# Linear attention with two branches on one core: query units of both branches in pairs of PSUM banks, single chunks of one weight load, and the last heads of both branches side by side

## The chip, the cores and the metric

The kernel runs on one core of a Trainium2 chip. The metric is the device time of one execution in microseconds (us); lower is better. All runs were fast, with a granted TensorE clock of 1.0. Within one call the kernels run on the same chip and share the runs of the kernel before. Each kernel was profiled in one of its executions; where profiles are compared below, it is one execution against one. A ratio is the mean time of a kernel's fast runs over the mean of the fast runs of the kernel before in the same rounds, with a 95% interval; it is therefore not quite the ratio of the medians that stand beside it. The span of a profile is about 1.3 us shorter than the time of the same run.

## The reference, cut to what matters

```python
# x: [1, 2048, 640] bf16; two branches A and B with their own wqkv [640, 1920] and wo [640, 640]; 32 heads of 20
g = sigmoid((x * gate_w).sum(-1, keepdims=True))
def branch(x, wqkv, wo):
    q, k, v = ...                                  # [1, 32, 2048, 20] each
    phi = lambda t: where(t > 0, t + 1, exp(t)) + 1e-6
    pq, pk = phi(q), phi(k)
    kv = einsum("bhsd,bhse->bhde", pk, v);  z = einsum("bhsd->bhd", pk)
    num = einsum("bhqd,bhde->bhqe", pq, kv)
    den = einsum("bhqd,bhd->bhq", pq, z)[..., None] + 1e-6
    return (num / den) merged over heads @ wo
return g * branch(A) + (1 - g) * branch(B)
```

## The kernel before

The work on TensorE goes in this order: keys of both branches (k), the products of phi(k) with x (g), the small products with the values (m), their products with wo (wp), then the queries in four blocks of 512 positions (q), the denominators (den), and the output matmuls (final). The wp rows go through DRAM to change their layout: WS is stored to the DRAM tensor wrows and loaded back as WPA or WPB. The reciprocal of the denominators takes the same road: RC is written to the DRAM tensor factor and read back as RX, spread over the heads. VectorE then multiplies phi(q) by RX.

The instructions are not written in the order in which an engine runs them. The kernel has its own list scheduler. At build time it gives each operation a duration from a small model, gives each engine a fixed order, and reserves PSUM banks. On the chip every engine runs its fixed order, and waits where a semaphore is late.

```python
WPLAG = 2

# loading of B's key weights: three transfers of 1, 2 and 2 chunks
for c0, c1 in ((0, 1), (1, 3), (3, 5)):
    dma("SP", "wkB%d" % c0, WK["B"][:, c0:c1, :], weights("B", D, c0, c1), writes=[...], us=0.55 * (c1 - c0))

def q_unit(X, b, k):                       # one branch, one PSUM bank, 512 columns
    tile = _Tile(1)
    ...
    mms("q%s%d%d" % (X, b, k), steps, [...], [(tile,)], NC * 518, after=gone[X])
    sch.op("ACT", ... e.activation(ek(), PS[:, tile.banks[0], :], ACT.Exp) ...)
    sch.op("DVE", ... e.tensor_scalar(ek(), ek(), 1.0, EPS, op0=ALU.min, op1=ALU.add) ...)
    sch.op("DVE", ... e.scalar_tensor_tensor(out=dst, in0=PS[...], scalar=0.0, in1=ek(), op0=ALU.max, op1=ALU.add) ...)

def wp_rows(X):                            # wsX, stored earlier by wp_store, holds the other rows
    dma("SP", "ws5" + X, ...)
    dma("SP", "wp" + X, WP[X][:, :, :], ..., reads=[("WD", X, 0), ("WD", X, 5)], writes=[("WP", X, k) for k in range(NC)], us=2.2)

def scale_q(b, dtile, pieces):
    sch.op("ACT", ... DN ...)              # copy the denominators out of PSUM
    sch.op("DVE", rec, 1740, ...)          # RC = 1 / DN
    dma("SP", "fw%d" % b, ...)             # factor <- RC
    dma("SP", "fr%d" % b, ..., reads=[("FD", b)], writes=[(xs,)], us=0.6)      # RX <- factor
    for j in range(pieces):
        for X in XS:
            sch.op("DVE", ... PQ[X] *= RX ...)

def queries(b):
    for X in XS:
        for k in range(NC):
            q_unit(X, b, k)
            q = 5 * (X == "B") + k - WPLAG
            if b == 1 and 0 <= q < 6:
                wp_unit("B", (q - 1) % 6)
                if q == 0: wp_rows("A")

queries(0); m_unit("B"); queries(1)
wp_store("B"); wp_rows("B")
d01 = dens(0); scale_q(0, d01, 2)
queries(2); queries(3)
...
```

## Time and profile before

| | |
|---|---|
| time, median | 190.74 us (190.50 to 191.07, 6 runs) |
| span of the profiled run | 189.7 us |
| TensorE / VectorE / ScalarE busy | 186.3 / 130.1 / 76.4 us |
| TensorE without a gap | 9.39 to 187.26 us |

The page of the kernel before, busy times and the chain that ended last:

```profile
PE 186.3 (98%) x1289; PEld 124.0 (65%) x1289; DVE 130.1 (69%) x275; ACT 76.4 (40%) x129; POOL 8.2 (4%) x14
PE 94%; DMA 3%; SPq 1%; DVE 0%; issue 0%; DVEq 0%
```

The chain in order of time (start, duration, what):

```profile
3.55 5.80 DMA WK<-in_B_wqkv_dram
...
9.39 177.87 PE ps L383 x1241
```

The busy share proves little by itself, because matmuls overlap and their ends are modelled. The starts do better. The timeline of TensorE in the queries (start, duration, engine, line, operation, operands, count):

```profile
95.31 5.56 PE L383 MATMUL ps<-XT,WQA 128*128 128x512 bf16 x25
100.71 5.56 PE L383 MATMUL ps<-XT,WQB 128*128 128x512 bf16 x25
```

25 matmuls of 512 columns start within 100.71 - 95.31 = 5.40 us, 216 ns each. The Trainium skill, "TensorE: Matmul & The Clock Gate", section "Wait — 56ns, not 53.3ns?", puts a warm matmul at its columns over 2.4 GHz plus about 2.5 ns, 215.8 ns here; the trace agrees. So TensorE is at this floor in the queries, and the chain shows no gap of it from 9.39 to 187.26 us.

SyncE issues the transfers of this stage, in a fixed order (start and duration of the issue, not of the transfer):

```profile
118.72 0.34 SPq L372 DMA_DIRECT2D wrowsB<-WS  x1
123.72 0.35 SPq L372 DMA_DIRECT2D WPB<-wrowsB  x1
125.59 2.31 SPq L372 DMA_DIRECT2D factor<-RC  x2
128.70 1.70 SPq L372 DMA_DIRECT2D RX<-factor  x2
```

And VectorE, where the multiplies of block 0 stand between the sums of the query units:

```profile
129.82 1.28 DVE L752 SCALAR_TENSOR_TENSOR FE<-ps,EK 128x512 bf16<-128x512 f32 x2
131.47 3.03 DVE L811 TENSOR_TENSOR FE<-FE,RX 128x1280 bf16<-128x1280 bf16 x4 [0.37 <-DMA RX<-factor]
134.42 0.49 DVE L747 TENSOR_SCALAR EK<-EK 128x512 bf16<-128x512 bf16 x2
```

The bracket says that VectorE stood idle for 0.37 us before the multiplies, until RX had landed. TensorE felt nothing of it: its matmuls show no late start there.

### The profile page before, as it was taken

The numbers are of one execution on the slowest core, as the hardware profiler recorded it, in microseconds if no ns is written. First come the engines' busy times: TensorE is split into PE (matmuls) and PEld (weight loads), VectorE is DVE, ScalarE is ACT, GpSimd is POOL, SyncE is SP. The second block draws the span as 40 slices with busy tenths as digits, with TensorE's granted clock in tenths as the row PEclk, the third lists the DMA queues.
The fourth block names the chain that finished last, engine by engine and source line by source line (L and its number), as shares of the span: only waits on it lengthen the run. The fifth ranks groups of instructions, "written<-read, shape, count | busy, mean of one in ns | idle before, by whom it ended". The sixth has DMA issues, their size and how long they took to land.

```text
span 189.7 us, 3209 instructions
## 1 busy us (share of the span) xinstructions
PE 186.3 (98%) x1289; PEld 124.0 (65%) x1289; DVE 130.1 (69%) x275; ACT 76.4 (40%) x129; POOL 8.2 (4%) x14
## 2 busy tenths in 40 slices
PE   8999999999999999999999999999999999999995
PEld 3565555555788888888855666455556677777774
DVE  1398989898600009996179997899999959833324
ACT  2255555555311112203255478565553522331332
POOL 8900000000000000000000000000000000000000
DMA  6999699991011111112144004665000173211212
GB/s 184 282 229 202 183 381 371 352 241 43 0 35 38 35 35 38 35 35 38 35 86 111 5 22 173 165 223 171 0 0 3 43 228 92 97 66 46 73 69 69
DMA packets 31936, 21.49 MB, mean 113 GB/s; under 512 B 16818, under 2 KB 31666, under 8 KB 31922
## 3 DMA queue, kind: packets, MB, share of 16 engines
q1 hardware_dynamic: 31490, 20.80, 39.4%
q10 hardware_dynamic: 432, 0.49, 0.8%
q8 instruction: 10, 0.16, 0.4%
q14 instruction: 4, 0.03, 0.1%
HBM read 12.05 MB, written 5.31 MB: 91 GB/s over the span
## 4 chain that ended last, share of the span: by engine, by line
PE 94%; DMA 3%; SPq 1%; DVE 0%; issue 0%; DVEq 0%
PE ps L383 94%; DMA WK<-in_B_wqkv_dram 3%; SPq L372 1%; DVE OL L862 0%; DVEq L276 0%
## 5 line engine op out<-in xcount | busy, mean ns | idle before, releaser
L383 PE MATMUL ps<-WK,XT 128*128 128x512 bf16 (+2 forms) x250 | 44.1, 337 | 0.4 <-DMA WK<-in_B_wqkv_dram 0.2
L383 PE MATMUL ps<-XN,FE 128*128 128x320 bf16 x320 | 44.3, 300 | 0.0
L383 PEld LDWEIGHTS ps<-XN,FE 128*128 128x128 bf16 x320 | 37.5, 117 | 6.0
L383 PEld LDWEIGHTS ps<-WK,XT 128*128 128x128 bf16 x250 | 24.0, 98 | 20.2 <-DMA WK<-in_B_wqkv_dram 1.1
L743 ACT ACTIVATE EK<-ps 128x512 bf16<-128x512 f32 x40 | 23.9, 597 | 18.4 <-PE ps L383 17.4
L563 ACT ACTIVATE EK<-ps 128x512 bf16<-128x512 f32 (+1 forms) x42 | 21.4, 526 | 16.2 <-PE ps L383 16.2
L752 DVE SCALAR_TENSOR_TENSOR FE<-ps,EK 128x512 bf16<-128x512 f32 x40 | 26.8, 688 | 0.7
L856 ACT ACTIVATE TS<-ps,GA 128x640 f32<-128x640 f32 (+2 forms) x18 | 13.1, 735 | 29.3 <-PE ps L383 29.3
L383 PE MATMUL ps<-WPB,FE 128*128 128x320 bf16 (+1 forms) x165 | 24.5, 295 | 0.0
L383 PE MATMUL ps<-WPA,FE 128*128 128x320 bf16 (+1 forms) x165 | 24.5, 295 | 0.0
L573 DVE SCALAR_TENSOR_TENSOR FE<-ps,EK 128x512 bf16<-128x512 f32 (+1 forms) x42 | 23.9, 597 | 0.5
L862 DVE SCALAR_TENSOR_TENSOR OS<-ps,GA,TS 128x640 bf16<-128x640 f32 x15 | 13.0, 870 | 15.2 <-PE ps L383 15.2
L383 PE MATMUL ps<-XT,WQA 128*128 128x512 bf16 x100 | 22.8, 380 | 0.0
L383 PE MATMUL ps<-XT,WQB 128*128 128x512 bf16 x100 | 22.7, 379 | 0.0
L600 ACT ACTIVATE GS<-ps 128x640 bf16<-128x640 f32 x10 | 7.0, 704 | 37.0 <-PE ps L383 37.0
L383 PEld LDWEIGHTS ps<-WPA,FE 128*128 128x128 bf16 x165 | 16.0, 98 | 6.2
L383 PEld LDWEIGHTS ps<-WPB,FE 128*128 128x128 bf16 x165 | 15.8, 98 | 6.2 <-ACT TS L856 0.4
L383 PEld LDWEIGHTS ps<-XT,WQB 128*128 128x128 bf16 x100 | 11.7, 117 | 9.2
L383 PEld LDWEIGHTS ps<-XT,WQA 128*128 128x128 bf16 x100 | 11.6, 118 | 9.4 <-issue 0.4
L705 DVE SCALAR_TENSOR_TENSOR GP<-XN,GWB 128x640 bf16<-128x640 bf16 x16 | 13.3, 828 | 4.1 <-PE ps L383 3.6
L567 DVE TENSOR_SCALAR EK<-EK 128x512 bf16<-128x512 bf16 (+1 forms) x42 | 11.4, 272 | 3.1
L811 DVE TENSOR_TENSOR FE<-FE,RX 128x1280 bf16<-128x1280 bf16 (+1 forms) x20 | 12.6, 686 | 0.9 <-DMA RX<-factor 0.9
(52 smaller groups left out, 80.8 us busy)
## 6 DMA issues: line engine op xcount, KB each, us to landing
out_dram<-OS SPq DMA_DIRECT2D x15, 160.0 KB, 1.8
XN<-in_A_x_dram SPq DMA_DIRECT2D x3, 640.0 KB, 8.4
factor<-RC SPq DMA_DIRECT2D x4, 256.0 KB, 2.6
RX<-factor SPq DMA_DIRECT2D x4, 256.0 KB, 3.0
WVA<-in_A_wqkv_dram SPq DMA_DIRECT2D x1, 800.0 KB, 10.8
WQA<-in_A_wqkv_dram SPq DMA_DIRECT2D x1, 800.0 KB, 12.2
WVB<-in_B_wqkv_dram SPq DMA_DIRECT2D x1, 800.0 KB, 11.2
WQB<-in_B_wqkv_dram SPq DMA_DIRECT2D x1, 800.0 KB, 12.2
```

The costliest lines, as they stand in the source:

```text
L372: ins = e.dma_start(dst() if callable(dst) else dst, src() if callable(src) else src, transpose=transpose)
L383: ins = pe.matmul(o, l, r, start=a, stop=z, tile_position=tp, skip_group_check=True)
L563: "ACT", lambda e, ps=ps, ek=ek: e.activation(ek(), ps(), ACT.Exp), _act_ns(n), reads=[(tile,)], writes=[(es,)],
L567: "DVE", lambda e, ek=ek: e.tensor_scalar(ek(), ek(), 1.0, EPS, op0=ALU.min, op1=ALU.add), _dve_ns(n, 4),
L573: return e.scalar_tensor_tensor(out=out, in0=two(ps()), scalar=0.0, in1=two(ek()), op0=ALU.max, op1=ALU.add)
L600: "ACT", lambda e: e.activation(GS[:, k, :].rearrange("p (h f) -> p h f", f=HALF), pair(tile, HALF), ACT.Copy),
L705: lambda e, t=t: e.scalar_tensor_tensor(out=GP[:, :], in0=XN[:, t, 0:D], scalar=1.0, in1=GWB[:, :], op0=ALU.mult, op1=ALU.mult, accum_out= ...
L743: "ACT", lambda e: e.activation(ek(), PS[:, tile.banks[0], :], ACT.Exp), _act_ns(512), reads=[(tile,)],
L752: lambda e: e.scalar_tensor_tensor(out=dst, in0=PS[:, tile.banks[0], :], scalar=0.0, in1=ek(), op0=ALU.max, op1=ALU.add),
L811: return e.tensor_tensor(out=v, in0=v, in1=RX[:, xs.slot, 512 * x + w * j : 512 * x + w * j + w].unsqueeze(1).to_broadcast([128, NC, w]), ...
L856: "ACT", lambda e: e.activation(t_ap(), acc(), ACT.Copy, scale=GA[:, 0, t : t + 1]), _act_ns(hi - lo),
L862: lambda e: e.scalar_tensor_tensor(out=o_ap(), in0=acc(), scalar=GA[:, 1, t : t + 1], in1=t_ap(), op0=ALU.mult, op1=ALU.add),
```

## The change

Its intent is to save work on VectorE and ScalarE with fewer, larger instructions, to let TensorE start on the first chunks of B's key weights sooner, and to run ten small matmuls in pairs. The diff has five parts, cut to their core:

```diff
-WPLAG = 2
+WPAT = ((1, 0), (1, 1), (1, 2), (1, 3), (1, 4), (2, 0))
 # 1. single chunks of B's WK, on two issuing engines
-        for c0, c1 in ((0, 1), (1, 3), (3, 5)):
-            dma("SP", "wkB%d" % c0, ...)
+        for c in range(NC):
+            load_wk(("SP", "ACT")[c % 2], "B", c)
 # 2. query units of A and B together: two banks, one Exp, one clamp, one sum
-        def q_unit(X, b, k):
-            tile = _Tile(1)
+        def q_pair(b, k):
+            tile = _Tile(2)
+            ... 10 matmuls, 5 for each branch, then Exp, clamp and sum of 1024 columns
 # 3. the last heads (40 columns) of A are computed with B's, side by side on two halves of the array
-                        for g in (0, 1) if q < 5 else (last,):
+                r = [step(X, tiles[0], q, g, j) for q in range(5) for j in range(NC) for g in (0, 1)]
+                if X == "B":
+                    r += [step(Y, tiles[1 - g], 5, g, j) for j in range(NC) for g, Y in enumerate(XS)]
 # 4. the wp units of B: one behind each of six pairs, in place of one behind each of six single units
-                    q = 5 * (X == "B") + k - WPLAG
-                    if b == 1 and 0 <= q < 6:
-                        wp_unit("B", (q - 1) % 6)
+                q_pair(b, k)
+                for i, p in enumerate(WPAT):
+                    if p == (b, k):
+                        wp_unit("B", (i - 1) % 6)
+                        if i == 5:
+                            wp_store("B")
+                            wp_rows("B")
 # 5. denominators copied out at once; the scaling of block 0 listed behind the queries of block 2
-        d01 = dens(0)
-        scale_q(0, d01, 2)
+        d0, d1 = dens(0)
         queries(2)
+        scale_q(0, d0, 2)
```

More of the change, by code (lines that the diff above doesn't have):

```diff
@@ L409, in load_x, with load_wk @@
             dma(eng, "xn%d" % t, XN[:, t, 0:D], xin[128 * t : 128 * t + 128, :], writes=[("XN", t)], us=0.25)
-        def load_wk(eng, c):
-            dma(eng, "wkA%d" % c, WK["A"][:, c, :], weights("A", D, c, c + 1)[:, 0, :], writes=[("WK", "A", c)], us=0.25)
+        def load_wk(eng, X, c):
+            dma(eng, "wk%s%d" % (X, c), WK[X][:, c, :], weights(X, D, c, c + 1)[:, 0, :], writes=[("WK", X, c)], us=0.25)
         load_x("SP", 0)
-        load_wk("ACT", 0)
+        load_wk("ACT", "A", 0)
         load_x("SP", 1)
-        load_wk("ACT", 1)
-        load_wk("SP", 2)
-        load_wk("ACT", 3)
-        load_wk("SP", 4)
-        for c0, c1 in ((0, 1), (1, 3), (3, 5)):
-            dma(
-                "SP", "wkB%d" % c0, WK["B"][:, c0:c1, :], weights("B", D, c0, c1), writes=[("WK", "B", c) for c in range(c0, c1)],
-                us=0.55 * (c1 - c0),
-            )
+        load_wk("ACT", "A", 1)
+        load_wk("SP", "A", 2)
+        load_wk("ACT", "A", 3)
+        load_wk("SP", "A", 4)
+        for c in range(NC):
+            load_wk(("SP", "ACT")[c % 2], "B", c)
         for t0, t1 in ((2, 4), (4, 8), (8, 12), (12, 16)):
@@ L484, in transpose_x @@
                 )
-        ring = {"ek": _Ring(NEK), "dn": _Ring(2), "rx": _Ring(2), "os": _Ring(NOS), "ts": _Ring(NTS)}
+        ring = {"ek": _Ring(NEK), "eq": _Ring(NEK // 2), "dn": _Ring(2), "rx": _Ring(2), "os": _Ring(NOS), "ts": _Ring(NTS)}
         def phi_k(X, t, tile):
@@ L622, in m_unit, with step, mask @@
         def m_unit(X):
-            tile = _Tile(1)
-            last = XS.index(X)
-            def steps():
-                r = []
-                for q in range(6):
-                    w = 12 if q < 5 else 8
-                    for j in range(NC):
-                        for g in (0, 1) if q < 5 else (last,):
-                            at = D * j + 120 * q + 60 * g * (q < 5)
-                            r.append((
-                                PS[64 * g : 64 * g + 64, tile.banks[0], 60 * q : 60 * q + NC * w], WV[X][:, at : at + 64],
-                                GT[X][:, j, :, 24 * q + 12 * g * (q < 5) : 24 * q + 12 * g * (q < 5) + w], j == 0, j == NC - 1, (0, 64 * g),
-                            ))
-                return r
-            mms("m%s" % X, steps, [("GT", X, k) for k in range(NC)] + [("WV", X), ("WVP", X)], [(tile,)], 25 * 75 + 400)
-            for q0, q1, g, w in ((0, 5, 0, 12), (0, 5, 1, 12), (5, 6, last, 8)):
+            tiles = [_Tile(1)] + [_Tile(1)] * (X == "B")
+            def step(Y, tile, q, g, j):
+                w, lo = (12, 12 * g) if q < 5 else (8, 0)
+                at = D * j + 120 * q + DH * lo // 4
+                return (
+                    PS[64 * g : 64 * g + 64, tile.banks[0], 60 * q : 60 * q + NC * w], WV[Y][:, at : at + 64],
+                    GT[Y][:, j, :, 24 * q + lo : 24 * q + lo + w], j == 0, j == NC - 1, (0, 64 * g),
+                )
+            def steps():
+                r = [step(X, tiles[0], q, g, j) for q in range(5) for j in range(NC) for g in (0, 1)]
+                if X == "B":
+                    r += [step(Y, tiles[1 - g], 5, g, j) for j in range(NC) for g, Y in enumerate(XS)]
+                return r
+            ys = XS if X == "B" else ("A",)
+            mms(
+                "m%s" % X, steps, [("GT", Y, k) for Y in ys for k in range(NC)] + [("WV", Y) for Y in ys] + [("WVP", Y) for Y in ys],
+                [(t,) for t in tiles], (len(tiles) + 9) * 190 + 240,
+            )
+            parts = [(0, 0, 5, 0, 12), (0, 0, 5, 1, 12)]
+            if X == "B":
+                parts = [(1, 5, 6, 0, 8), (0, 5, 6, 1, 8)] + parts
+            for i, q0, q1, g, w in parts:
                 n = DH * (w // 4)
-                def mask(e, q0=q0, q1=q1, g=g, w=w, n=n):
+                def mask(e, i=i, q0=q0, q1=q1, g=g, w=w, n=n):
                     p0 = 64 * g
@@ L648, in mask @@
                         out=MB[p0 : p0 + n, q0:q1, 60 * g : 60 * g + n].rearrange("p q (i k) -> p q k i", k=NC),
-                        in0=PS[p0 : p0 + n, tile.banks[0], 60 * q0 : 60 * q0 + n * (q1 - q0)].rearrange("p (q k i) -> p q k i", k=NC, i=w),
+                        in0=PS[p0 : p0 + n, tiles[i].banks[0], 60 * q0 : 60 * q0 + n * (q1 - q0)].rearrange(
+                            "p (q k i) -> p q k i", k=NC, i=w
+                        ),
                         in1=m.unsqueeze(1).to_broadcast([n, q1 - q0, NC, w]), op=ALU.mult,
@@ L653, in m_unit @@
                 sch.op(
-                    "DVE", mask, _dve_ns(n * (q1 - q0)), reads=[(tile,), ("CB",)], writes=[("M", q) for q in range(q0, q1)],
+                    "DVE", mask, _dve_ns(n * (q1 - q0)), reads=[(tiles[i],), ("CB",)], writes=[("M", q) for q in range(q0, q1)],
                     name="mm%s" % X,
@@ L722, in gates, with eq, eq2 @@
             )
-        def q_unit(X, b, k):
-            tile = _Tile(1)
-            es = _Tile(1, ring["ek"])
-            def ek():
-                return EK[:, es.slot, 0:512]
-            dst = PQ[X][:, k, 512 * b : 512 * b + 512]
+        def q_pair(b, k):
+            tile = _Tile(2)
+            es = _Tile(1, ring["eq"])
+            def eq():
+                return EK[:, :, :].rearrange("p n f -> p (n f)")[:, 1280 * es.slot : 1280 * es.slot + 1024]
+            def eq2():
+                return eq().rearrange("p (x s) -> p x s", x=2)
+            dst = FE[:, :, S * k + 512 * b : S * k + 512 * b + 512]
@@ L732, in q_unit @@
             span = range(S * k + 512 * b, S * k + 512 * b + 512)
-            over = [("F", X, w, t) for w in ("k", "k5") for t in range(span[0] // D, span[-1] // D + 1)]
+            over = [("F", X, w, t) for X in XS for w in ("k", "k5") for t in range(span[0] // D, span[-1] // D + 1)]
             def steps():
                 return [
-                    (PS[:, tile.banks[0], :], WQ[X][:, c, k : D : NC], XT[:, c, 512 * b : 512 * b + 512], c == 0, c == NC - 1, None)
-                    for c in range(NC)
-                ]
@@ L741, in q_unit @@
-            mms("q%s%d%d" % (X, b, k), steps, [("XTC", t, c) for t in range(4 * b, 2) for c in range(NC)] + [("XT", t) for t in range(max(2, 4 * b), 4 * b + 4)] + [("WQ", X)], [(tile,)], NC * 518, after=gone[X])
+                    (PS[:, tile.banks[x], :], WQ[X][:, c, k : D : NC], XT[:, c, 512 * b : 512 * b + 512], c == 0, c == NC - 1, None)
+                    for x, X in enumerate(XS) for c in range(NC)
+                ]
+            xt = [("XTC", t, c) for t in range(4 * b, 2) for c in range(NC)] + [("XT", t) for t in range(max(2, 4 * b), 4 * b + 4)]
@@ L742, in q_unit @@
+            o = mms("q%d%d" % (b, k), steps, xt + [("WQ", X) for X in XS], [(tile,)], 2 * NC * 518, after=gone["B"])
+            sch.op("ACT", lambda e: e.activation(eq2(), pair(tile, 512), ACT.Exp), _act_ns(1024), reads=[(tile,)], writes=[(es,)], name="eq%d%d" % (b, k))
             sch.op(
-                "ACT", lambda e: e.activation(ek(), PS[:, tile.banks[0], :], ACT.Exp), _act_ns(512), reads=[(tile,)],
-                writes=[(es,)], name="eq%s%d%d" % (X, b, k),
+                "DVE", lambda e: e.tensor_scalar(eq(), eq(), 1.0, EPS, op0=ALU.min, op1=ALU.add), _dve_ns(1024, 4),
+                reads=[(es,)], writes=[(es,)], name="tq%d%d" % (b, k),
@@ L745, in q_unit @@
             )
             sch.op(
-                "DVE", lambda e: e.tensor_scalar(ek(), ek(), 1.0, EPS, op0=ALU.min, op1=ALU.add), _dve_ns(512, 4),
-                reads=[(es,)], writes=[(es,)], name="tq%s%d%d" % (X, b, k),
-            )
-            sch.op(
-                "DVE",
-                lambda e: e.scalar_tensor_tensor(
-                    out=dst, in0=PS[:, tile.banks[0], :], scalar=0.0, in1=ek(), op0=ALU.max, op1=ALU.add
-                ),
-                _dve_ns(512), reads=[(tile,), (es,)], writes=[("PQ", X, k, b)] + over, name="sq%s%d%d" % (X, b, k),
-            )
+                "DVE", lambda e: e.scalar_tensor_tensor(out=dst, in0=pair(tile, 512), scalar=0.0, in1=eq2(), op0=ALU.max, op1=ALU.add),
@@ L758, in dens @@
+                _dve_ns(1024), reads=[(tile,), (es,)], writes=[("PQ", X, k, b) for X in XS] + over, name="sq%d%d" % (b, k),
+            )
+            return o
         def dens(b0):
@@ L778, in dens, with scale_q @@
             )
-            return dtile
-        def scale_q(b, dtile, pieces):
-            ds = _Tile(1, ring["dn"])
-            lo = 256 * (b % 2)
-            sch.op(
-                "ACT",
-                lambda e: e.activation(DN[:, ds.slot, :], PS[:, dtile.banks[0], lo : lo + 256], ACT.Identity, bias=EP[:, 0:1]), _act_ns(256),
-                reads=[(dtile,), ("EP",)], writes=[(ds,)], name="dn%d" % b,
-            )
+            ds = []
+            for b in (b0, b0 + 1):
+                d = _Tile(1, ring["dn"])
+                ds.append(d)
+                sch.op(
+                    "ACT",
+                    lambda e, d=d, lo=256 * (b - b0): e.activation(
+                        DN[:, d.slot, :], PS[:, dtile.banks[0], lo : lo + 256], ACT.Identity, bias=EP[:, 0:1]
+                    ),
+                    _act_ns(256), reads=[(dtile,), ("EP",)], writes=[(d,)], name="dn%d" % b,
+                )
+            return ds
+        def scale_q(b, ds, pieces):
             def rec(e):
@@ L919, in queries @@
         def queries(b):
-            for X in XS:
-                for k in range(NC):
-                    q_unit(X, b, k)
-                    q = 5 * (X == "B") + k - WPLAG
-                    if b == 1 and 0 <= q < 6:
-                        wp_unit("B", (q - 1) % 6)
-                        if q == 0:
+            for k in range(NC):
+                q_pair(b, k)
+                for i, p in enumerate(WPAT):
+                    if p == (b, k):
+                        wp_unit("B", (i - 1) % 6)
+                        if i == 0:
                             wp_rows("A")
+                        if i == 5:
+                            wp_store("B")
+                            wp_rows("B")
         def finals(b):
@@ L938, in bass_gated_mix__linear_attn_block__linear_attn_block__prompt_kernel @@
         queries(1)
-        wp_store("B")
-        wp_rows("B")
-        d01 = dens(0)
-        scale_q(0, d01, 2)
+        d0, d1 = dens(0)
         queries(2)
+        scale_q(0, d0, 2)
         queries(3)
-        scale_q(1, d01, 2)
-        d23 = dens(2)
+        scale_q(1, d1, 2)
+        d2, d3 = dens(2)
         finals(0)
-        scale_q(2, d23, 2)
+        scale_q(2, d2, 2)
         finals(1)
-        scale_q(3, d23, 4)
+        scale_q(3, d3, 4)
         finals(2)
```

## The prediction

> **What bounds the kernel.** TensorE. The chain of waits has one unbroken piece of TensorE work, 177.87 of 189.7 us, from 9.39 to 187.26; before it 5.8 us of WK-of-B DMA, after it about 2.4 us of output. The page's busy share (98%) proves little, since matmul ends are modelled, so I used start-to-start times in the timeline: 25 query matmuls of 512 columns take 5.40 us (216 ns each), ten output matmuls of 320 columns 1.358 us (136 ns). The Trainium skill, "TensorE: Matmul & The Clock Gate", section "Wait — 56ns, not 53.3ns?", gives N/2.4 GHz plus about 2.5 ns for a warm matmul: 215.8 and 135.8 ns; the trace agrees. So after 9.39 us TensorE runs at its own rate; only fewer matmuls or a shorter start save time.
>
> **The change, costed.**
> 1. Query pairs. Still 200 matmuls of 512 columns, 43.2 us. From the groups, Exp takes 384/597/702 ns at 256/512/640 columns, the sum 415/688/825, the clamp 227/288/336. Estimates at 1024: Exp 1.02 us, clamp 0.42, sum 1.23. ScalarE saves 20 x 0.17 = 3.4 us, VectorE 20 x 0.30 = 6 us, both off the chain: VectorE is 96-99% busy at 120-150 us, yet TensorE does not wait there. Worth 0.
> 2. Cost of pairs: a pair is held for 2.16 us of matmuls plus about 3 us of Exp, clamp, sum and handover: 5.2 us against 2.16 us between pairs, so 2.4 of 4 pairs in use. With the m tiles, a wp tile or a den bank one pair less is left, when masks (1.03 us each) or reciprocals (1.75) come between. I allow 0 to 1 us of new TensorE stalls near 106-110, 120-123 and 142-148 us; expected 0.2.
> 3. Single WK chunks. TensorE loses 0.21, 0.31 and 0.41 us (late starts at 6.75, 8.43, 9.39) to WK. Chunks of 160 KB land about 0.45 us apart, so bytes, not issue, set the pace; two issuing engines share the same 16 DMA engines (the skill, "DMA: Bandwidth & Descriptors", section "Issuing engines are not separate DMA queues"). B's last byte stays near 9.3 us. But today chunks 3 and 4 land together at 9.345 and 14 matmuls follow; with single chunks 12 follow: 2 x 136 ns = 0.27 us saved, on the chain.
> 4. Last heads side by side. Five single 40-column matmuls start 32 ns apart in each branch; side by side two take those 32 ns. 5 x 32 = 0.16 us saved, on the chain.
> 5. wp of B ends later (near 121 us); WPB's way through DRAM (about 5 + 4 us) still ends before its use near 144 us.
>
> Sum: -0.27 - 0.16 + 0.2 = about -0.25; I say 190.4 us, 8 in 10 between 189.7 and 191.3. Faster by over 2%: 0.01; within 2%: 0.97; slower: 0.02.
>
> **Signs.** Right: query pairs 2.16 us apart; Exp near 1.02, sum near 1.23 us; VectorE busy near 124 us, ScalarE near 73; last B chunk landing at 9.0 to 9.6 us, then twelve 320-column matmuls. Wrong: TensorE waiting on VectorE or ScalarE inside 95-150 us for over 0.5 us in all (step 2), B's last chunk landing before 8.9 or after 9.8 us (step 3), a wait on WPB before the final matmuls (step 5).
>
> **What would upset it.** The kernel's list scheduler orders work by its own cost model; a badly placed mask or reciprocal could stall several pairs.

## The result, and the profile after

The kernel after takes 192.88 us in the median (191.86 to 193.56, 6 runs), the kernel before 190.74 us. The ratio is 1.0105 (1.0074 to 1.0137). So it is slower by about 1%, less than 2%, but outside the range of the prediction (189.7 to 191.3). Its runs also scatter three times as widely: 1.7 us against 0.6. The profiled run was the fastest of the six, with a span of 190.5 us.

The page of the kernel after:

```profile
PE 185.6 (97%) x1280; PEld 124.2 (65%) x1289; DVE 125.7 (66%) x235; ACT 73.0 (38%) x109; POOL 8.2 (4%) x14
PE 88%; DMA 6%; DVE 4%; issue 1%; ACT 0%; DVEq 0%
```

ScalarE saves what was forecast (3.4 us) and VectorE 4.4 us of the 6 forecast, and the chain now leaves TensorE. In order of time:

```profile
125.40 1.75 DVE RC L802
127.15 1.08 DVE FE L759
128.23 0.05 DVE EK L755
128.28 5.13 DMA factor<-RC
133.40 0.02 issue
133.42 2.78 DMA RX<-factor
136.20 0.02 issue
136.22 3.04 DVE FE L820 x4
139.26 0.67 DVE EK L755 x2
139.93 1.14 DVE FE L759
141.07 0.05 issue
141.12 7.79 PE ps L383 x50
```

Read it from the bottom. At 141.12 TensorE starts a query pair that waited for two free banks. They came free with the sum of an earlier pair (L759, ending at 141.07), that sum stood behind the four multiplies of block 0 (L820), and these waited for RX. RX waited for the write of the factor, which took 5.13 us. (The chain names VectorE, L759 and L755, for the 1.13 us before that write. The write needs neither: what ended at 128.23 was also SyncE's issue before it, as the SyncE view below shows.) The timeline of TensorE shows what it cost:

```profile
137.75 1.24 PE L383 MATMUL ps<-XT,WQA 128*128 128x512 bf16 x5
138.83 1.24 PE L383 MATMUL ps<-XT,WQB 128*128 128x512 bf16 x5
141.12 1.27 PE L383 MATMUL ps<-XT,WQA 128*128 128x512 bf16 x5 [1.05 <-DVE FE L759]
```

Five matmuls from 138.83 on take 5 x 216 ns, so the next could have started at 139.91. It starts 1.21 us later. (A group that shows x4, followed by a start 216 ns late, is a missing record and no gap; I don't count those.) VectorE and SyncE of the kernel after, in the same stage:

```profile
133.34 1.23 DVE L759 SCALAR_TENSOR_TENSOR FE<-ps,EK 128x1024 bf16<-128x1024 f32 x1
136.22 3.04 DVE L820 TENSOR_TENSOR FE<-FE,RX 128x1280 bf16<-128x1280 bf16 x4 [1.66 <-DMA RX<-factor]
139.17 0.76 DVE L755 TENSOR_SCALAR EK<-EK 128x1024 bf16<-128x1024 bf16 x2
```

```profile
122.89 0.34 SPq L372 DMA_DIRECT2D wrowsB<-WS  x1
127.88 0.35 SPq L372 DMA_DIRECT2D WPB<-wrowsB  x1
128.28 2.57 SPq L372 DMA_DIRECT2D factor<-RC  x2
133.42 1.12 SPq L372 DMA_DIRECT2D RX<-factor  x2
```

The store of B's rows is issued at 122.89 instead of 118.72, since its last wp unit now comes behind the first pair of block 2. SyncE can issue the load of WPB only when those rows have landed, at 127.88. The write of the factor is next in SyncE's order: RC was ready at 127.15 (end of L802 in the chain), but the write is issued at 128.28. Then the write and the load of WPB are under way together. The packets of the trace say how: from 128.3 to 131.6 the DMA engines moved packets of the load alone (109, none under 2 KB), and the write's 512-byte packets began at 131.64. So the write stood behind the load's data in SyncE's DMA queue, more than it moved beside it.

Counted from the first den matmul, RX of block 0 lands after 131.45 - 121.99 = 9.46 us in the kernel before, and after 136.20 - 123.58 = 12.62 us in the kernel after. The difference of 3.16 us has three parts: the write is issued 1.10 us later on this scale (4.70 against 3.60), it takes 2.04 us more (5.13 against 3.09), and the read is nearly the same (2.78 against 2.75).

### The profile page after: what moved, and what is told of

It is laid out like the page before. It is cut to its first block, busy times and chain, and to the rows that moved or that the text cites. A ratio compares the mean times of both kernels' runs of the same rounds, so it can differ in the third digit from the quotient of the medians.

```text
span 190.5 us, 3131 instructions
## 1 busy us (share of the span) xinstructions
PE 185.6 (97%) x1280; PEld 124.2 (65%) x1289; DVE 125.7 (66%) x235; ACT 73.0 (38%) x109; POOL 8.2 (4%) x14
## 4 chain that ended last, share of the span: by engine, by line
PE 88%; DMA 6%; DVE 4%; issue 1%; ACT 0%; DVEq 0%
PE ps L383 87%; DMA factor<-RC 3%; DMA XN<-in_A_x_dram 2%; DVE FE L820 2%; DMA RX<-factor 1%; DVE FE L759 1%; DVE RC L802 1%; PE ps L468 1%; DVE EK L755 0%; DVE OL L871 0%; ACT DN L791 0%; DVEq L276 0%
## 5 line engine op out<-in xcount | busy, mean ns | idle before, releaser
L753 ACT ACTIVATE EK<-ps 128x1024 bf16<-128x1024 f32 x20 | 20.5, 1023 | 24.0 <-PE ps L383 21.9
L383 PE MATMUL ps<-XT,WQA 128*128 128x512 bf16 x95 | 24.0, 379 | 1.6 <-DVE FE L759 1.0
L383 PE MATMUL ps<-XT,WQB 128*128 128x512 bf16 x100 | 24.8, 379 | 0.0
L759 DVE SCALAR_TENSOR_TENSOR FE<-ps,EK 128x1024 bf16<-128x1024 f32 x20 | 24.3, 1217 | 0.4
L820 DVE TENSOR_TENSOR FE<-FE,RX 128x1280 bf16<-128x1280 bf16 (+1 forms) x20 | 12.7, 688 | 3.4 <-DMA RX<-factor 3.4
```

What stands on the lines that cost most here:

```text
L383: ins = pe.matmul(o, l, r, start=a, stop=z, tile_position=tp, skip_group_check=True)
L753: sch.op("ACT", lambda e: e.activation(eq2(), pair(tile, 512), ACT.Exp), _act_ns(1024), reads=[(tile,)], writes=[(es,)], name="eq%d%d" % ( ...
L759: "DVE", lambda e: e.scalar_tensor_tensor(out=dst, in0=pair(tile, 512), scalar=0.0, in1=eq2(), op0=ALU.max, op1=ALU.add),
L820: return e.tensor_tensor(out=v, in0=v, in1=RX[:, xs.slot, 512 * x + w * j : 512 * x + w * j + w].unsqueeze(1).to_broadcast([128, NC, w]), ...
```

## The experiments

The theory that came out of this reading, T1: the late wp units hold up the factor, its lateness blocks VectorE's fixed order, and that costs TensorE a gap. The rivals: T2, a pair of banks is simply too coarse for eight banks, wherever the factor lands; T3, the start scatters with two issuing engines for the key weights.

### First call: the same kernel again, an earlier wp, a later multiply, and a late wp in the kernel before

**x1_after_again** is the kernel after, unchanged.

> The changed kernel, unchanged, to see a second execution. Theory T1 (late factor): the multiplies of block 0 stand ahead of the query clamps in VectorE's fixed order and wait for the factor that comes back from DRAM late, so TensorE runs out of PSUM pairs near 141 us. Then the TensorE gap near 141 us should vary with the landing of the factor, and be 1.2 to 3 us, and account for all of the excess over the kernel before: median 192.3 to 193.4. Rival T2 (pairs as such are too coarse for eight banks): the gap is the same in each execution, about 1.2 us, wherever the factor lands. Rival T3 (the start scatters with two issuing engines): the excess is found before 50 us, where the g matmuls start later than 49.2 us.

Median 192.66 us, ratio 1.0086 (1.0068 to 1.0105). In its profile RX lands 12.42 us after the first den matmul and the gap near 141 us is 1.00 us. With the first profile (12.62 and 1.21) that is a difference of 0.20 in the landing and 0.21 in the gap. Expected was a gap of 1.2 us or more; it is smaller, but it moves with the landing, as T1 has it. The gap does not account for all of the excess: the g matmuls also start at 49.61 us instead of 49.16 (but at 48.74 in the first profile of the kernel after), so a part of T3 is alive.

**x2_wp_e2** brings the wp units forward.

```diff
-WPAT = ((1, 0), (1, 1), (1, 2), (1, 3), (1, 4), (2, 0))
+WPAT = ((1, 0), (1, 1), (1, 1), (1, 2), (1, 2), (1, 3))
```

> The changed kernel with the six wp units of B put at pairs (1,0),(1,1),(1,1),(1,2),(1,2),(1,3) instead of one at each of six pairs, so that WPB is written and loaded some 5 us earlier and is out of the factor's way. T1: WPB lands near 127 to 128 us, the factor is written in about 3 us instead of 5.1, VectorE waits under 0.5 us for it, no TensorE gap over 0.3 us near 141 us; 190.0 to 190.5 us. T2 (pairs too coarse): the gap of about 1.2 us stays, 191.5 us or more. T3: no change from the kernel after, about 192.9.

Median 192.34 us, ratio 1.0063 (1.0046 to 1.0080): a miss in the time. The gap near 141 us is gone, with RX 9.08 us after den, as T1 said. VectorE did not wait for RX of block 0 at all (the 1.6 us in its list of waits belong to a later block, at 159 us). WPB landed at 130.28, later than expected, and the scheduler also moved one of the four multiplies before one sum. But two wp units in a row, each with a pair of banks of its own, opened a new gap at 114 us, 0.82 us by the starts:

```profile
112.87 0.71 PE L383 MATMUL ps<-WOB,MB 124*120 124x320 bf16 x4
114.24 1.27 PE L383 MATMUL ps<-XT,WQA 128*128 128x512 bf16 x5 [0.66 <-DVE FE L759]
```

And this execution lost 2.15 us at the start, to a chunk of A's key weights that landed at 8.04 us. So the edit traded one gap for another, and its time tests T1 neither way.

**x3_ml_late** changes one number of the scheduler's model, so that the multiplies of block 0 are placed later among the query pairs. It moved them behind two more pairs (17 query sums stand before them, 15 in the kernel after), not one as the expectation says; the order of the transfers in this stage stays.

```diff
-                reads=[("FD", b)], writes=[(xs,)], us=0.6,
+                reads=[("FD", b)], writes=[(xs,)], us=4.6 if b == 0 else 0.6,
```

> The changed kernel with one number of its scheduler's model changed (the read of factor 0 planned at 4.6 instead of 0.6 us), which moves the four multiplies of block 0 behind one more query pair in VectorE's order and touches no transfer. T1: the factor still lands late (about 136 us), but VectorE has clamps and sums to do until then; TensorE gap near 141 us below 0.4 us; 190.1 to 191.0 us. T2: gap stays; 191.5 us or more, since pairs, banks and VectorE's total work are the same. T3: no change from the kernel after.

Median 191.22 us, 0.2 us above the expected window, ratio 1.0008 (0.9988 to 1.0027), against 1.0086 for the kernel after on the same chip in the same rounds. RX is as late as ever, 12.63 us after den, and the write of the factor took 5.14 us. But VectorE has two more clamps and sums to do meanwhile, and waits for nothing before the multiplies:

```profile
137.89 0.43 DVE L755 TENSOR_SCALAR EK<-EK 128x1024 bf16<-128x1024 bf16 x1 [0.47 <-ACT EK L753]
138.35 1.23 DVE L759 SCALAR_TENSOR_TENSOR FE<-ps,EK 128x1024 bf16<-128x1024 f32 x1
139.49 3.02 DVE L820 TENSOR_TENSOR FE<-FE,RX 128x1280 bf16<-128x1280 bf16 x4
```

TensorE goes on without a gap:

```profile
139.81 1.24 PE L383 MATMUL ps<-XT,WQB 128*128 128x512 bf16 x5
140.89 1.24 PE L383 MATMUL ps<-XT,WQA 128*128 128x512 bf16 x5
141.97 1.24 PE L383 MATMUL ps<-XT,WQB 128*128 128x512 bf16 x5
143.05 1.52 PE L383 MATMUL ps<-WPA,FE 128*128 128x320 bf16 x10
```

The pairs, the banks and VectorE's total work are those of the kernel after. T2 falls as the cause, and the gap was worth about 0.8% of the time, some 1.5 us.

**x4_before_wp_late** does the opposite: the kernel before, single banks, with only the wp units made late.

```diff
-                    q = 5 * (X == "B") + k - WPLAG
-                    if b == 1 and 0 <= q < 6:
+                    n = 10 * (b - 1) + 5 * (X == "B") + k
+                    if n in (1, 3, 5, 7, 9, 11):
+                        q = n // 2
                         wp_unit("B", (q - 1) % 6)
+                        ... wp_store("B") and wp_rows("B") behind the last, as in the change
```

> The kernel before (single banks, 40 units) with the wp units of B spread as late as in the change, at every second query unit from the second of block 1 into block 2. T1, if the lateness alone does it: RX of block 0 lands after 134 us instead of 131.4, VectorE waits 1.5 us or more for it, and TensorE stalls by 0.5 to 2 us near 135 to 143 us, 191.2 to 192.8 us. If lateness needs the pairs to hurt (T2 in part): VectorE waits as long but TensorE has no gap over 0.2 us, 190.6 to 191.0 us.

Median 193.41 us, ratio 1.0126 (1.0100 to 1.0153), more than expected. RX lands 13.86 us after den, and VectorE waits 2.8 us:

```profile
132.72 0.69 DVE L752 SCALAR_TENSOR_TENSOR FE<-ps,EK 128x512 bf16<-128x512 f32 x1
136.22 3.03 DVE L811 TENSOR_TENSOR FE<-FE,RX 128x1280 bf16<-128x1280 bf16 x4 [2.80 <-DMA RX<-factor]
```

TensorE starts late by 0.28 us at 140, 0.25 and 0.16 at 145 to 147, and 0.67 us more than usual at 149, together about 1.4 us. The single banks spread the loss over more places, but do not save it. This edit also has a fault of its own: its first wp unit comes one query unit too early and waits 0.95 us for a mask at 110 us, which explains why the total is above the expectation. The scheduler also put the multiplies behind two more query sums, and the lateness came about in another way than in the kernel after: the write was issued on time (3.60 us after den) but took 5.08 us beside the store of B's rows, and the read took 5.16 us beside the load of WPB. So x4 shows that the lateness is enough to do harm without any pairs; its size is not a clean measure.

### Second call: the loading of the key weights

**y1_before_wk_chunks** is the kernel before with only the single chunks, as in the change (0, 2, 4 on SyncE, 1, 3 on ScalarE). **y2_before_wk_sp** has single chunks on SyncE alone.

```diff
-        for c0, c1 in ((0, 1), (1, 3), (3, 5)):
-            dma("SP", "wkB%d" % c0, ...)
+        for c in range(NC):
+            dma(("SP", "ACT")[c % 2], "wkB%d" % c, WK["B"][:, c, :], ..., us=0.25)     # y1; in y2 all "SP"
```

> The kernel before with only the loading of B's WK changed: single chunks, 0, 2, 4 issued by SyncE and 1, 3 by ScalarE. Theory S1 (the second issuing engine holds A's chunks up and scatters the start): the last WK chunk of B lands between 9.1 and 10.3 us, in the mean later than the 9.0 to 9.3 of the old loading, the g matmuls start 0 to 1 us later than 49.2, and the median is 190.9 to 191.7 us, with a wider spread than before. The prediction's theory S0: 12 instead of 14 matmuls behind the last chunk, 190.5 us.

> The kernel before with single chunks of B's WK, all issued by SyncE. S1: no more transfers on ScalarE's queue than before, so the old arrival of A's chunks and the last B chunk at 9.0 to 9.4 us, only 12 matmuls behind it: 190.3 to 190.7 us. If the splitting itself costs (more transfers), the last chunk lands after 9.6 us and the time is 190.9 us or more.

y1: median 190.65 us (189.99 to 191.41), ratio 0.9997 (0.9973 to 1.0021). y2: 190.38 us, ratio 0.9986 (0.9969 to 1.0004). Neither can be told from the kernel before. The 0.27 us that the prediction gave y1 did not show, and neither did the loss that I expected of y1 (190.9 us or more); only the spread is wider, 1.4 us against 0.8. In y2 the last chunk landed at 8.55 us, earlier than expected.

**y3_after_wk_before** is the kernel after with the old loading.

```diff
-        for c in range(NC):
-            load_wk(("SP", "ACT")[c % 2], "B", c)
+        for c0, c1 in ((0, 1), (1, 3), (3, 5)):
+            dma("SP", "wkB%d" % c0, ...)
```

> The kernel after with the old loading of B's WK; pairs, late wp and everything else as in the change. If the excess is a late-factor stall of about 1.1 us (T1) and a start that costs about 0.5 to 0.7 us (S1), then the stall near 141 us stays, 1.0 to 1.6 us, and the time lies at 191.6 to 192.2 us, between the two kernels. If the start is not at fault it stays at 192.7.

Median 192.35 us, a little above the window, ratio 1.0082 (1.0063 to 1.0100). The slowness stays almost whole, so T3 is not its main cause. The gap was larger than I expected in this execution, 1.89 us by the starts, with RX landing 13.31 us after den:

```profile
139.10 1.24 PE L383 MATMUL ps<-XT,WQB 128*128 128x512 bf16 x5
142.07 1.27 PE L383 MATMUL ps<-XT,WQA 128*128 128x512 bf16 x5 [1.72 <-DVE FE L762]
```

**y4_ml_late_wk_sp** joins x3 with the loading of y2.

> The kernel after with the multiplies of block 0 moved behind one more query pair (as in x3) and B's WK in single chunks on SyncE alone. T1 and S1 together: no TensorE gap over 0.2 us between 95 and 150 us, old start minus two matmuls, minus 0.16 us for the last heads: 190.1 to 190.6 us, below the kernel before. If the pairs cost something else that has not been found, 190.9 us or more.

Median 190.61 us (189.94 to 190.88), ratio 0.9987 (0.9969 to 1.0005); no gap over 0.1 us between 95 and 145 us apart from the usual starts of m and den. The median is a hair above the expected window. With the pairs in, the kernel is level with the kernel before.

### Third call: why the factor is late

**z1_wpb_pool** changes one word: GpSimd, idle at that time, issues the load of WPB. The order on all other engines is the same.

```diff
-                "SP", "wp" + X, WP[X][:, :, :], ...
+                "POOL" if X == "B" else "SP", "wp" + X, WP[X][:, :, :], ...
```

> The changed kernel with one word changed: the load of WPB is issued by GpSimd, idle then, instead of SyncE. All other orders are the same. It tells apart two reasons why the factor comes back late: SyncE standing before the WPB load until the rows of B have landed, with the factor's write behind it (about 1.1 us in the profile after), and the two transfers sharing the DMA engines (write of the factor 5.1 us instead of 3.1). If the standing in line alone does it: RX of block 0 lands 11.4 us or less after the first den matmul, gap near 141 us under 0.3 us, 191.0 to 191.4. If both count: the gap shrinks by about 1.1 us but 0 to 0.8 stay, 191.2 to 191.9. If only sharing counts: gap as before, 192.5.

Median 191.58 us, in the window given for both reasons together, ratio 1.0051 (1.0028 to 1.0074). SyncE no longer stands before the WPB load, and issues the factor 1.09 us earlier on the scale of den (127.53 - 123.92 = 3.61 us):

```profile
123.24 0.34 SPq L372 DMA_DIRECT2D wrowsB<-WS  x1
127.53 3.67 SPq L372 DMA_DIRECT2D factor<-RC  x2
131.24 3.87 SPq L372 DMA_DIRECT2D RX<-factor  x2
```

The write is done before the WPB load gets going (2.66 us), but now the read shares the engines with it and takes 4.24 us (131.24 to 135.49) instead of 2.78. The read also stood in line once more: its factor had landed at 130.19, but SyncE's order puts the write of the second factor first (one of the x2 above), and that had to wait for its reciprocal until 130.68. RX lands 11.56 us after den (3.61 + 2.66 + 1.05 in line + 4.24) and the gap shrinks to 0.14 us. So both count, standing in line and the load's data in the way, and which transfer pays for the latter depends on when WPB moves. The Trainium skill, "DMA: Bandwidth & Descriptors", section "Issuing engines are not separate DMA queues", says that transfers from any engine run on the same 16 DMA engines and interleave; this trace agrees (WPB's packets, in GpSimd's queue, run from 130.12 to 133.59 us, and the 512-byte packets of SyncE's queue start among them at 132.61). The same page, section "Anatomy of one DMA — SWDGE (gpsimd) path", says that DMA engines do not wait on semaphores and that any such wait happens on the issuing sequencer before dispatch. The section is about transfers that GpSimd issues; the traces agree with it for SyncE: in the kernel after it issues the load of WPB at 127.88, 0.06 us after B's rows landed. The standing in line is that wait, with the factor behind it. The time of this kernel holds 0.5 us more outside the span than all the others (time minus span 1.81 to 1.86 us against 1.25 to 1.37), so the ratio understates what the edit does inside it.

**z2_wpb_behind** puts the load of WPB behind the factor of block 0, on SyncE; the wp units stay late. (The scheduler, told of the new order, also moved one of the four multiplies before one sum, and the read of the first factor now comes before the write of the second.)

```diff
-                        wp_rows("B")
+                        wp_rows("B", load=False)
 ...
         scale_q(0, d0, 2)
+        wp_load("B", extra=[("RXD", 0)])       # RXD 0 is written by the read of RX, block 0
```

> The changed kernel with the load of WPB put behind the factor of block 0 (it waits until RX has landed), all on SyncE; wp units stay late. Nothing stands before the factor and nothing moves beside it: the write takes about 2.6 us, RX lands about 9 us after the first den matmul (12.4 to 13.3 in the late executions), no TensorE gap over 0.2 us at 135 to 145 us, WPB still lands before 142 us: 190.4 to 191.2 us. If the gap stays, the lateness of the factor is not the cause.

Median 191.22 us, a hair above the expected window, ratio 1.0025 (1.0003 to 1.0046). SyncE now issues:

```profile
128.11 0.61 SPq L372 DMA_DIRECT2D factor<-RC  x1
130.76 0.39 SPq L372 DMA_DIRECT2D RX<-factor  x1
131.27 0.53 SPq L372 DMA_DIRECT2D factor<-RC  x1
133.54 0.34 SPq L372 DMA_DIRECT2D WPB<-wrowsB  x1
```

The write takes 2.64 us, RX lands 8.96 us after den, there is no gap, and WPB lands at 137.88, 6.5 us before its use at 144.36. VectorE does not wait for RX of block 0 (the 1.8 us in its list of waits belong to a later block, at 158 us). Against z1 the new order of the read is a part of the gain (1.05 us there). In the kernel after the old order cost nothing, since the second write was issued before the first had landed.

**z3_wp_e4_wk_sp** has the last two wp units one pair earlier and the loading of y2; **z4_wpb_behind_wk_sp** is z2 with the loading of y2.

```diff
-WPAT = ((1, 0), (1, 1), (1, 2), (1, 3), (1, 4), (2, 0))
+WPAT = ((1, 0), (1, 1), (1, 2), (1, 3), (1, 3), (1, 4))      # z3
```

> The changed kernel with wp units of B at (1,0),(1,1),(1,2),(1,3),(1,3),(1,4), the last one pair earlier than in the change and only one pair with two, and B's WK in single chunks on SyncE. The store of B's rows starts about 2.2 us earlier, so the load of WPB is issued before the factor is ready. Expected: no 0.8 us gap as in x2, RX 10 to 11.3 us after the first den matmul, gap near 141 us under 0.2 us: 190.1 to 190.8 us.

> z2 with B's WK in single chunks on SyncE: candidate for the best kernel. 190.0 to 190.6 us, 0.1 to 0.3 per cent under the kernel before; pairs cost nothing once the factor is in time.

z3: median 190.81 us (190.14 to 191.16), ratio 1.0002 (0.9978 to 1.0026), RX 10.10 us after den, no gap at 114 or 141 us in its profile; the median is just outside the expected window. z4: 190.49 us (189.81 to 190.95), ratio 0.9989 (0.9965 to 1.0013), RX 9.14 us after den, no gap.

### What the runs say together

The profiles with the multiplies in the place that the change gave them (all four together before the two delayed pairs), by the landing of RX after the first den matmul:

| run | RX after den, us | gap near 141 us, us | landing minus gap, us |
|---|---|---|---|
| z1 | 11.56 | 0.14 | 11.42 |
| x1 | 12.42 | 1.00 | 11.42 |
| after | 12.62 | 1.21 | 11.41 |
| y3 | 13.31 | 1.89 | 11.42 |

In these four, from 11.56 to 13.31 us, what goes past 11.42 us is lost by TensorE one for one; z3, with one of the four multiplies one sum earlier, lands at 10.10 us and has no gap. And in x3 and y4, where the multiplies stand two pairs later, 12.63 and 12.75 us cost nothing. That settles T1. In the last three rows the landing moves by 0.9 us from one execution to the next, and the gap moves with it. This may be a part of the wide scatter of the kernel after, but no run shows that: x1, the same kernel, scattered by 0.6 us only, and y1, without this gap, by 1.4.

The pairs as such cost nothing. From the first query matmul to the first final matmul z3 takes 141.71 - 94.34 = 47.37 us, the kernel before 142.64 - 95.31 = 47.33 us.

The start stays half open. The last chunk of B's key weights landed between 9.09 and 10.25 us in the seven profiles with two issuing engines (mean 9.75), between 8.55 and 9.63 in the four with single chunks on SyncE (9.07), and at 8.92 to 9.35 in the three with the old loading (9.09). The g matmuls started at 49.50, 48.87 and 49.00 us in the mean. That points to a cost of two issuing engines of about 0.5 us, with a scatter of 1.6 us between executions. With two engines TensorE's longer waits were not for the last chunk of B, though, but for the first. SyncE issues it, and it landed at 8.10 to 9.32 us, behind the second chunk, which ScalarE issues; with B's chunks on SyncE alone (single or old loading, seven profiles) it landed at 6.71 to 7.89. The first 20 key matmuls of B stand behind it. They started 0.23 to 0.78 us late in five of the seven profiles with two engines (x1, x3, y1, z1, z2), and not late in the seven with one. In the times, single chunks on SyncE against two engines gave 0.9986 against 0.9997 (y2, y1) and 0.9989 against 1.0025 (z4, z2), and y3 against the kernel after is within the intervals. By these intervals no difference is clear of noise, though the means of z2 and z4 (191.20 and 190.47 us, six runs each in the same rounds) lie 0.73 us apart with a standard error of 0.22. Why the chunks land later with two engines, no run here shows.

## Why the prediction was wrong, point by point

- **What bounds the kernel:** right. TensorE at its own rate, and anything that takes it off that rate is lost.
- **Step 1, savings off the chain:** right in worth and, but for VectorE's total (4.4 us saved, said: 6), in size. Exp took 1.023 us, the clamp 0.42, the sum 1.217; ScalarE is busy 73.0 us (said: near 73), VectorE 125.7 (said: near 124). The 4.4 us that VectorE saved bought nothing, because TensorE had not waited for it.
- **Step 2, stalls from pairs:** this is the step that failed. I allowed "0 to 1 us of new TensorE stalls", "expected 0.2". Measured were 1.21, 1.00 and 1.89 us at one place, 141 to 142 us. Removing the gap took the ratio from 1.0086 to 1.0008 (x3). The reason given was wrong too: banks held longer and masks or reciprocals between were not at fault (x3, z2 and y4 keep all of these). I named the sign beforehand, TensorE waiting on VectorE for over 0.5 us, and it showed.
- **Step 5, the late wp of B:** the step that hid the cause. "WPB's way through DRAM ... still ends before its use" is true: it landed at 132.6 us and was used at 144.67. But I asked only when WPB is needed, not what stands behind it in SyncE's order and what it shares the DMA engines with. The factor's write was issued 1.10 us later and took 2.04 us more because of it. z1 and z2 show both: take WPB out of SyncE's line and the issue comes 1.09 us earlier; put it behind the factor altogether and the write takes 2.64 us and the read 2.71.
- **Step 3, single chunks:** "B's last byte stays near 9.3 us" and 0.27 us saved. The matmul count was right (in y4 and z4 TensorE's last late start of this stage, 0.09 us, has 12 matmuls behind it), but with two issuing engines the last chunk landed at 9.75 us in the mean, and three of seven profiles were past my limit of 9.8. And the wait was at the wrong chunk: in five of the seven TensorE stood 0.23 to 0.78 us for B's first chunk, which I had not asked about. y1 alone measured 0.9997, no gain that can be told from noise.
- **Step 4, last heads side by side:** right. The m stage of A fell from 1.05 to 0.91 us by the starts, 0.14 us, and that of B did not grow (1.06 us in z1 as before).
- **What would upset it:** I named the list scheduler and "a badly placed mask or reciprocal". It was a badly placed multiply, and the scheduler's model of a transfer was what misplaced it: it plans the read of a factor with 0.6 us of engine time, and its fixed order cannot react when the transfer is late.

## What to carry to other kernels

When a change delays a transfer, don't ask only whether its own consumer still gets it in time; list what follows it on the same issuing engine and what moves beside it, and ask who waits for those. In a fixed order, an instruction that waits for DRAM belongs behind enough other work to cover the worst landing: moving four multiplies by two pairs won back about 1.5 us here, and moving one load behind a more urgent one closed the same gap. A saving on an engine that nobody waits for is worth nothing: the 4.4 us of VectorE here bought no time.

## What the Trainium skill lacked or had wrong

- "Perfetto Trace Analysis", section "Identifying the Most-Contended Engine", names MFU (the share of the peak arithmetic rate) and the busy share of LDWEIGHTS as the measures of TensorE's headroom. Here the weight loads are busy 65% in both kernels, with and without the gap, although the kernel before shows no gap of TensorE from 9.39 to 187.26 us; the start-to-start times of the matmuls (216 ns at 512 columns) told it, and also showed the gap. MFU was not worked out.
- "DMA: Bandwidth & Descriptors", section "Issuing engines are not separate DMA queues", says that more issuing engines save only issue time. The page puts a transfer's wait on the issuing sequencer, but doesn't draw the consequence that a transfer that waits for data holds up the later transfers of its engine: 1.10 us here, and 1.09 us back by one issue on GpSimd.
- The same section does not warn that the chunks of a load can land later when two engines issue: B's first chunk at 8.10 to 9.32 us against 6.71 to 7.89 with one (seven profiles each; cause open).
- None of the pages named here has it: the one kernel in which GpSimd issued a transfer showed 1.81 to 1.86 us between its span and its time, all the others of these calls 1.25 to 1.37 us.
